# Gates and inputs at another address, and a chunk's end split differently between ScalarE and VectorE

## The chip, the cores and the metric

One core of a Trainium2 chip runs the whole program. The metric is the device time of one execution in microseconds; a kernel's time is the median of several executions. The engines are named as in the profile: PE is TensorE (matrix products; PEld its weight loads), DVE is VectorE, ACT is ScalarE, POOL is GpSimd, SP is SyncE, which issues all DMAs here. Matrix products write to PSUM, eight banks of 128 partitions by 512 float32; all other tiles lie in SBUF.

## The reference

Attention with a band mask over q, k and v (batch 4, 8 heads, 768 positions, head width 64): a query sees the first 8 positions and the 96 up to its own, a bias falls with the distance, and the softmax is taken over what is kept. The result, 3072 rows of 512, goes through a feed-forward net:

```python
h = x @ w_in                     # 3072x512 by 512x2048
g = np.maximum(0.01 * h, h)
return (g @ w_out).astype(np.float32)   # 3072x2048 by 2048x512
```

The weights are float64 at the start and all products are wanted at more than one pass's accuracy, so the kernel splits each operand into a high and a low part and adds three products: high by high, high by low, low by high.

## The kernel before, in words

The 24 blocks of 128 rows are taken in eleven chunks: two of three blocks (chunks 0 and 1) and nine of two (chunks 2 to 10). Attention runs ahead of the feed-forward net in small events (lines 192 to 330: scores, softmax, transposes, product with v). While chunks 0 and 1 run (lines 885 to 908), the weights are still being converted, into four tiles that stay for the whole program: `wih`, `wil` for the first product and `woh`, `wol` for the second.

From chunk 2 on, a chunk is eight steps p = 0 to 7, each for 256 of the 2048 hidden columns. In loop pass s the program does `hidden_pair(s)` (L449: 24 products of 256 columns with `xh`, `xl` as the moving operand and `wih`, `wil` as the weights loaded into the array), then `gates(s)`, then `out_pair(s - 2)`, the second product for the step two passes earlier (L493). `gates` copies the PSUM result to SBUF on ACT (`t`, L460), takes the leaky maximum on DVE (L461), casts the high part on ACT (`gh`, L468) and subtracts for the low part on DVE (`gl`, L469).

Where the first result lands alternates: even passes write `ps_h`, odd passes the first half of the tile `ps_p`. The second product accumulates in five banks: `bank[3]` and `bank[4]` hold the sums for the chunk's two row blocks (`bank[4]` is the second half of `ps_p`), and `bank[1]`, `bank[2]` hold four half-width partial sums of the last three steps. In the second product `gh`, `gl` are the loaded weights, and `woh`, `wol` (moving) stream through, 512 columns at a time. Steps p = 5 to 7 of chunks 3 to 10 (`fast`) do it as seven products of halves instead of eight, with sums and differences of gates (L464) and of weight halves (`h`, `l`, made once in `prepare`); these stream 256 columns, and in two products of p = 5 the first pass streams 512. The five banks are then combined in `results(c)`, called after `out_pair` of p = 7, that is in pass p = 1 of the next chunk. The next chunk's p = 0 writes `bank[3]` first and `bank[4]` three products later, in the pass after that, and has to find both read out.

All of ACT, DVE and SP work in order of their queues. In this late part the order is not pinned: a scheduler lays it out when the program is built, by a simulated time. After the last chunk, a check of the inputs (L766 to L768: a product on PE into a bank that `ps_p` had, a reduction and a cast on DVE) sets a flag, which all engines load (L923) before the program ends.

Of the kernel before, what the change touches and what calls it, by code (L numbers as in the profile page):

```python
# [10 lines left out]
F32 = mybir.dt.float32  # L11
# [7 lines left out]
P = 128  # L19
# [12 lines left out]
PAIR = 2  # L32
# [19 lines left out]
def fast_path(ctx, tc, qp, kp, vp, wi, wo, nvec, weights, nmall, out, B, H, S):  # L52
    nc = tc.nc
# [9 lines left out]
    GT = P * PAIR  # L63
# [3 lines left out]
    const = ctx.enter_context(tc.tile_pool(name="const", bufs=1))  # L67
# [11 lines left out]
    ps_x = ctx.enter_context(tc.tile_pool(name="ps_x", bufs=1, space=bass.MemoryType.PSUM))  # L79


    one = const.tile([P, 16], F32, name="one")[:, :1]
    nc.vector.memset(one, 0.0)
    pinned_exp = nc.scalar.activation(out=one, in_=one, func=AF.Exp)
    tc.keep_in_program_order(pinned_exp)
# [20 lines left out]
    def pin(ins):  # L106

        if pinned[0]:
            tc.keep_in_program_order(ins)
# [362 lines left out]
    def fast(c, p):  # L472

        return c > STD and p >= NP - FAST

    def add(o, x, y, op=ALU.add):
        pin(nc.vector.tensor_tensor(out=o, in0=x, in1=y, op=op))  # L477

    def half_bank(n):
        return bank[1 + n // 2][:, n % 2 * GT:(n % 2 + 1) * GT]  # L480

    def out_pair(s):
# [29 lines left out]
        if end:  # L512
            results(c)

    def results(c):

        u = [late["ev"].tile([P, 2, GT], F32, tag="ev", name="part") for _ in range(PAIR)]
        r = [x.rearrange("p a b -> p (a b)") for x in u]
        if not fast(c, NP - 1):
            pin(nc.scalar.copy(out=r[0], in_=bank[3]))  # L520
            pin(nc.vector.tensor_copy(out=r[1], in_=bank[4]))
        else:
            pin(nc.scalar.copy(out=u[0][:, 0], in_=half_bank(1)))
            add(u[0][:, 1], u[0][:, 0], half_bank(0))
            add(u[1][:, 0], u[0][:, 1], half_bank(3))
            add(u[1][:, 1], u[1][:, 0], half_bank(2))
            add(u[0][:, 1], u[0][:, 1], half_bank(2))
            for n in range(PAIR):
                add(r[n], r[n], bank[3 + n])
        for n in range(PAIR):  # L530
            r0 = (first_step[c] + n) * P
            nc.sync.dma_start(out=out[r0:r0 + P, :], in_=r[n])

    def prepare(p):

        e, o = 2 * p, 2 * p + 1
        first = p == NP - FAST
        h = late["w"].tile([P, (4 if first else 3) * GT], F32R, tag=f"h{p}", name=f"h{p}")
        l = late["w"].tile([P, 3 * GT], F32R, tag=f"l{p}", name=f"l{p}")
        sides[p] = h, l  # L540
        x = [y[:, n] for y in (late["ev"].tile([P, 2, GT], F32, tag="ev", name="wk") for _ in range(3)) for n in range(2)]

        def block(to, f, n):
            cs = slice(n * GT, (n + 1) * GT)
            add(to, woh[:, f, cs].bitcast(F32), wol[:, f, cs].bitcast(F32))

        def split(v, dh, dl):
            pin(nc.scalar.copy(out=dh, in_=v))
            add(dl, v, dh.bitcast(F32), ALU.subtract)
        cols = [slice(n * GT, (n + 1) * GT) for n in range(4)]  # L550
        block(x[0], e, 1)
        block(x[1], e, 0)
        add(x[2], x[0], x[1], ALU.subtract)
        split(x[2], h[:, cols[0]], l[:, cols[0]])
        block(x[1], o, 1)
        add(x[3], x[1], x[0], ALU.subtract)
        split(x[3], h[:, cols[3 if first else 2]], l[:, cols[2]])
        add(x[0], x[1], x[2], ALU.subtract)
        split(x[0], h[:, cols[1]], l[:, cols[1]])
        block(x[4], o, 0)  # L560
        add(x[5], x[4], x[0], ALU.subtract)
        split(x[5], woh[:, e, GT:], wol[:, e, GT:])
        if first:
            pin(nc.vector.memset(x[4], 0.0))
            pin(nc.scalar.copy(out=h[:, cols[2]], in_=x[4]))
# [25 lines left out]
    late = {}  # L591
# [30 lines left out]
    bank = [ps_x.tile([P, 2, 512], F32, tag="ps_t", name="ps_p")]  # L622
    bank.extend(ps_o.tile([P, 2 * GT], F32, tag="ps_o", name="ps_m") for _ in range(3))
    bank.append(bank[0][:, 1])
    for s in range(NS + 2):
        for t in ev_pair.get(s, ()):
            event(t)
        if s < NS:
            hidden_pair(s)
        if s == 0:  # L630
            ffn2(len(order) - 1)
            later.close()
            for name, n in (("a", 2), ("ev", 3), ("w", 1)):
                late[name] = ctx.enter_context(tc.tile_pool(name=name, bufs=n))
        if s < NS:
            gates(s)
        if s >= 2:
            out_pair(s - 2)
        if NP + 2 <= s < NP + 2 + 2 * FAST and s % 2 == 0:
            prepare(NP - FAST + (s - NP - 2) // 2)  # L640
# [270 lines left out]
def tile_kernel(tc, a, out, B, H, S):  # L911
    nc = tc.nc
    NF, _, NK, _ = a["wi"].shape
    DM = a["wo"].shape[3]
    NB = S // P
    with tc.tile_pool(name="keep", bufs=1) as keep, tc.tile_pool(name="xs", bufs=1, space=bass.MemoryType.DRAM) as dram:
        nvec = read_counts(tc, keep, a["ngl"])
        nmall = keep.tile([P, B * NB * H], F32, name="nmall")
        weights = (keep.tile([P, NK, NF * P], F32R, name="wih"), keep.tile([P, NK, NF * P], F32R, name="wil"),
                   keep.tile([P, NF, DM], F32R, name="woh"), keep.tile([P, NF, DM], F32R, name="wol"))  # L920
        fast_path(tc, a["qp"], a["kp"], a["vp"], a["wi"], a["wo"], nvec, weights, nmall, out, B, H, S)
        with tc.tile_pool(name="fin", bufs=1) as fin:
            flag = nc.values_load(band_holds(tc, fin, nvec, nmall), min_val=0, max_val=1,  # L923
                                  skip_runtime_bounds_check_because="the flag is a product of comparisons")
        with tc.If(flag == 0):
            xs = dram.tile([B, S // 256, P, NK, 256], F32, name="xs")
            general_attention(tc, a["qt"], a["kt"], a["vt"], nvec, xs, B, H, S)
            general_ffn(tc, weights, xs, out)
# [50 lines left out]
```

## Time and profile before

| | before |
|---|---|
| time, median of 3 | 669.3 us (668.08 to 670.57) |
| profiled execution | 667.78 us, span 666.0 us, granted clock 0.993 |
| PE busy | 630.9 us (95%) |
| DVE busy | 420.8 us (63%) |
| ACT busy | 287.9 us (43%) |
| POOL busy | 82.4 us (12%) |

The span is what the trace covers, from the first instruction to the last. Busy time of PE counts overlapping products once, and the end of a product is modelled, so the pace of products is better read from one start to the next. Three views are used beside the page: the chain of waits, which follows the work that ended last back in time and merges neighbours ("x24"); the list of who waited for whom; and the timeline of one engine, whose rows have the start in us, the duration in us, engine, line and operation, and in brackets the idle time before with what ended it.

### The profile page before, as it was taken

Reading aid. Unit: us, or ns where it says so; the run is one execution under the profiler, and the core shown is the slowest. Engines: PE = TensorE matmul, PEld = TensorE weight load, DVE = VectorE, ACT = ScalarE, POOL = GpSimd, SP = SyncE. Lnnn points to the kernel's source line nnn. Section 1 sums busy time; section 2 is a strip of 40 time slices with the busy share of each in tenths; the row PEclk is TensorE's granted clock in tenths of the full one; section 3 lists DMA queues with packets and bytes.
Section 4 is the critical chain, followed back from the end, with each engine's and each line's share of the span. In section 5 each row is a group of like instructions: output and inputs, shape, how many; then the busy total and the mean of one; then the engine's idle time right before and its main releaser. Section 6 shows DMA issues by size and latency. Waiting matters only on the chain.

```text
span 666.0 us, 15916 instructions
## 1 busy us (share of the span) xinstructions
PE 630.9 (95%) x6275; PEld 558.4 (84%) x6275; DVE 420.8 (63%) x1202; ACT 287.9 (43%) x754; POOL 82.4 (12%) x147
## 2 busy tenths in 40 slices
PE   5769999999999999899999999999999999999995
PEld 4568889998888888798889889889889889889984
DVE  5989988885657537957467556556656656534443
ACT  5877754555434434434334334334334333322221
POOL 3434600000111000101001001001001000100000
PEclk9899999999999999999999999999999999999998
DMA  8786533422555425224434433423432531400001
GB/s 281 238 257 187 184 127 126 127 64 80 175 146 197 151 75 168 62 70 156 131 95 137 144 103 94 145 88 115 142 115 84 167 103 53 131 1 1 32 1 37
DMA packets 52098, 79.76 MB, mean 120 GB/s; under 512 B 7728, under 2 KB 27184, under 8 KB 52016
## 3 DMA queue, kind: packets, MB, share of 16 engines
q1 hardware_dynamic: 52016, 78.67, 37.1%
q8 instruction: 51, 0.84, 0.5%
q14 instruction: 31, 0.25, 0.1%
HBM read 59.51 MB, written 19.14 MB: 118 GB/s over the span
## 4 chain that ended last, share of the span: by engine, by line
PE 82%; DVE 7%; ACT 3%; DMA 2%; issue 2%; POOL 1%; SPq 1%; DVEq 0%; ACTq 0%; POOLq 0%
PE ps_m L493 18%; PE ps_p L449 15%; PE ps_h L449 13%; PE ps_p L493 12%; PE ps_av L324 4%; PE ps_av L192 3%; PE ps_h L885 3%; PE ps_o L908 3%; PE ps_o L907 3%; PE ps_o L906 3%; PE ps_h L887 3%; PE ps_h L886 3%; DVE part L477 2%; DMA kr<-in_kp_dram 2%; ACT pr L219 1%
## 5 line engine op out<-in xcount | busy, mean ns | idle before, releaser
L468 ACT CAST gh<-t 128x512 fp32r<-128x512 f32 (+1 forms) x72 | 52.3, 727 | 139.0 <-PE ps_p L493 86.9
L469 DVE TENSOR_TENSOR gl<-t,gh 128x512 fp32r<-128x512 f32 (+1 forms) x72 | 59.3, 823 | 79.7 <-ACT gh L468 74.8
L219 ACT ACTIVATE pr<-pr,nmall 128x192 f32<-128x192 f32 (+1 forms) x192 | 83.3, 435 | 18.4 <-DVE nmall L206 18.4
L461 DVE SCALAR_TENSOR_TENSOR t<-t 128x512 f32<-128x512 f32 x72 | 49.6, 689 | 61.8 <-ACT t L460 61.5
L449 PE MATMUL ps_p<-xh,wih 128*128 128x256 f32 x288 | 82.7, 287 | 0.0
L449 PE MATMUL ps_h<-xh,wih 128*128 128x256 f32 x288 | 80.6, 280 | 0.0
L449 PE MATMUL ps_p<-xh,wil 128*128 128x256 f32 x288 | 80.1, 278 | 0.0
L449 PE MATMUL ps_p<-xl,wih 128*128 128x256 f32 x288 | 80.0, 278 | 0.0
L449 PE MATMUL ps_h<-xh,wil 128*128 128x256 f32 x288 | 79.7, 277 | 0.0
L449 PE MATMUL ps_h<-xl,wih 128*128 128x256 f32 x288 | 79.7, 277 | 0.0
L48 POOL TENSOR_SCALAR xh<-x 128x256 fp32r<-128x256 f32 x48 | 22.0, 457 | 466.1 <-ACT x L330 383.0
L493 PE MATMUL ps_m<-woh,gh 128*128 128x512 f32 (+1 forms) x168 | 59.0, 351 | 4.3 <-DVE part L477 4.3
L449 PEld LDWEIGHTS ps_p<-xh,wih 128*128 128x128 f32 x288 | 54.1, 188 | 6.3 <-issue 5.7
L493 PE MATMUL ps_m<-woh,gl 128*128 128x512 f32 (+1 forms) x168 | 58.1, 346 | 0.0
L493 PE MATMUL ps_m<-wol,gh 128*128 128x512 f32 (+1 forms) x168 | 58.0, 345 | 0.0
L449 PEld LDWEIGHTS ps_h<-xh,wih 128*128 128x128 f32 x288 | 54.1, 188 | 3.0 <-issue 2.2
L206 DVE CUSTOM_DVE_ANT_0 pr<-ps_av,nbw 128x192 f32<-128x192 f32 x136 | 40.5, 354 | 24.0 <-ACT x L330 23.8
L449 PEld LDWEIGHTS ps_h<-xl,wih 128*128 128x128 f32 x288 | 54.1, 188 | 0.9
L449 PEld LDWEIGHTS ps_p<-xl,wih 128*128 128x128 f32 x288 | 54.1, 188 | 0.4
L449 PEld LDWEIGHTS ps_p<-xh,wil 128*128 128x128 f32 x288 | 54.4, 189 | 0.0
L449 PEld LDWEIGHTS ps_h<-xh,wil 128*128 128x128 f32 x288 | 54.1, 188 | 0.0
L493 PE MATMUL ps_p<-woh,gh 128*128 128x512 f32 (+1 forms) x120 | 46.5, 388 | 3.3 <-ACT t L460 2.7
(130 smaller groups left out, 1467.1 us busy)
## 6 DMA issues: line engine op xcount, KB each, us to landing
via<-pr SPq DMA_DIRECT2D x30, 384.0 KB, 2.5
pt_d<-via SPq DMA_DIRECT2D x120, 96.0 KB, 2.4
kr<-in_kp_dram SPq DMA_DIRECT2D x40, 256.0 KB, 3.7
vr<-in_vp_dram SPq DMA_DIRECT2D x40, 256.0 KB, 3.2
wst<-in_wi_dram SPq DMA_DIRECT2D x16, 512.0 KB, 3.6
wst<-in_wo_dram SPq DMA_DIRECT2D x16, 512.0 KB, 3.5
qs<-in_qp_dram SPq DMA_DIRECT2D x24, 256.0 KB, 3.9
out_dram<-part SPq DMA_DIRECT2D x21, 256.0 KB, 2.3
```

The costliest lines, as they stand in the source:

```text
L48: return eng.tensor_scalar(out=dst, in0=src, scalar1=1.0, scalar2=1.0, op0=ALU.mult, op1=ALU.mult)
L192: tc.keep_in_program_order(nc.tensor.matmul(own(u, av[qf, j, a * KW:(a + 1) * KW]), lhsT=q[rows, a, qf], rhs=keys(rows, a, f), start=True, ...
L206: pin(nc.vector.tensor_tensor_reduce(out=head(u, pr, a, j), in0=own(u, ps[:, j, a * KW:(a + 1) * KW]), in1=nb, scale=-0.125, scalar=3.0e38 ...
L219: pin(nc.scalar.activation(out=p, in_=p, func=AF.Exp, scale=-1.0, bias=nm[:, 2 * a + j:2 * a + j + 1], accum_out=sm[:, 2 * a + j:2 * a + j ...
L324: tc.keep_in_program_order(nc.tensor.matmul(av[out, a, cols], lhsT=v[rows, t, j, :], rhs=near(rows, j, t, fs), start=(n == 0), stop=(n == ...
L449: tc.keep_in_program_order(nc.tensor.matmul(o, lhsT=w[:, k, fs], rhs=x[:, k, :], start=(k + i == 0), stop=(k == NK - 1 and i == 2)))
L461: pin(nc.vector.scalar_tensor_tensor(out=g, in0=g, scalar=0.01, in1=g, op0=ALU.mult, op1=ALU.max))
L468: pin(nc.scalar.copy(out=gh[:, :n - a0], in_=t[:, a0:n]))
L469: pin(nc.vector.tensor_tensor(out=gl[:, :n - a0], in0=t[:, a0:n], in1=gh[:, :n - a0].bitcast(F32), op=ALU.subtract))
L493: tc.keep_in_program_order(nc.tensor.matmul(to, lhsT=x[:, a], rhs=y, start=first and n == 0, stop=last and n == 2))
L885: tc.keep_in_program_order(nc.tensor.matmul(ps, lhsT=wih[:, k, fs], rhs=xh[:, k, :CT], start=(k == 0), stop=False))
L886: tc.keep_in_program_order(nc.tensor.matmul(ps, lhsT=wih[:, k, fs], rhs=xl[:, k, :CT], start=False, stop=False))
```

## The change

First, a chunk's end. Before, ACT copies one half bank to SBUF and DVE does the rest: four additions of 256 columns that read PSUM, then two of 512 columns that add `bank[3]` and `bank[4]`. Now ACT copies `bank[3]` (512 columns), the half bank (256) and `bank[4]` (512), in this order in the text, and DVE does six additions of 256 columns, four of them with a PSUM operand, and one of 512 in SBUF. A third tile `u` is used beside the two result tiles.

Second, addresses. The first small tile of the pool `const` grows from 64 to 128 bytes a partition, which moves what is allocated after it from the same side by 64 bytes; `gap`, 64 bytes, moves the tiles `h`, `l` back. The addresses in the two built programs, modulo 128 bytes:

| tile | before | after |
|---|---|---|
| `wih`, `wil`, `woh`, `wol` | 0 | 0 |
| `xh`, `xl` of chunk 0 | 0 | 64 |
| `xh`, `xl` of chunks 1 to 10 | 64 | 64 |
| `gh`, `gl`, all chunks | 0 | 64 |
| `h`, `l` of `prepare` | 0 | 0 |
| q, k, v, `pr` of attention | 64 | 0 |
| `pt`, `dg` of attention | 0 | 64 |
| `pt_d` of attention | 64 | 64 |

```diff
-    one = const.tile([P, 16], F32, name="one")[:, :1]
+    one = const.tile([P, 32], F32, name="one")[:, :1]
 ...
     def results(c):
 
-        u = [late["ev"].tile([P, 2, GT], F32, tag="ev", name="part") for _ in range(PAIR)]
-        r = [x.rearrange("p a b -> p (a b)") for x in u]
+        r = [late["ev"].tile([P, 2, GT], F32, tag="ev", name="part") for _ in range(PAIR)]
+        rows = [x.rearrange("p a b -> p (a b)") for x in r]
+        pin(nc.scalar.copy(out=rows[0], in_=bank[3]))
         if not fast(c, NP - 1):
-            pin(nc.scalar.copy(out=r[0], in_=bank[3]))
-            pin(nc.vector.tensor_copy(out=r[1], in_=bank[4]))
+            pin(nc.vector.tensor_copy(out=rows[1], in_=bank[4]))
         else:
-            pin(nc.scalar.copy(out=u[0][:, 0], in_=half_bank(1)))
-            add(u[0][:, 1], u[0][:, 0], half_bank(0))
-            add(u[1][:, 0], u[0][:, 1], half_bank(3))
-            add(u[1][:, 1], u[1][:, 0], half_bank(2))
-            add(u[0][:, 1], u[0][:, 1], half_bank(2))
-            for n in range(PAIR):
-                add(r[n], r[n], bank[3 + n])
+            u = late["ev"].tile([P, 2, GT], F32, tag="ev", name="u")
+            pin(nc.scalar.copy(out=u[:, 0], in_=half_bank(1)))
+            pin(nc.scalar.copy(out=rows[1], in_=bank[4]))
+            add(r[0][:, 0], r[0][:, 0], u[:, 0])
+            add(u[:, 0], u[:, 0], half_bank(0))
+            add(u[:, 1], u[:, 0], half_bank(3))
+            add(u[:, 0], u[:, 0], half_bank(2))
+            add(r[1][:, 1], r[1][:, 1], half_bank(2))
+            add(r[0][:, 1], r[0][:, 1], u[:, 0])
+            add(r[1], r[1], u[:, 1].unsqueeze(1).to_broadcast([P, 2, GT]))
         for n in range(PAIR):
             r0 = (first_step[c] + n) * P
-            nc.sync.dma_start(out=out[r0:r0 + P, :], in_=r[n])
+            nc.sync.dma_start(out=out[r0:r0 + P, :], in_=rows[n])
 
     def prepare(p):
 
         e, o = 2 * p, 2 * p + 1
         first = p == NP - FAST
+        if first:
+            gap = late["w"].tile([P, 16], F32, tag="gap", name="gap")
+            nc.gpsimd.memset(gap, 0.0)
```

The scheduler lays out the late part anew. This is ACT at the end of chunk 3 (`part` are the result tiles, `t`, `gh` the gates of the next chunk, `ps_m` any of `bank[1]` to `bank[3]`), before:

```order
L460 COPY t<-ps_p 128x512
L523 COPY part<-ps_m 128x256
L468 CAST gh<-t 128x512
L460 COPY t<-ps_h 128x512
L468 CAST gh<-t 128x512
```

and after:

```order
L460 COPY t<-ps_p 128x512
L468 CAST gh<-t 128x512
L519 COPY part<-ps_m 128x512
L524 COPY u<-ps_m 128x256
L525 COPY part<-ps_p 128x512
L460 COPY t<-ps_h 128x512
L468 CAST gh<-t 128x512
```

The three copies stand behind the cast `gh` of pass p = 1 and ahead of the copy `t` of pass p = 2. On DVE at the same place, before:

```order
L461 SCALAR_TENSOR_TENSOR t<-t 128x512
L477 TENSOR_TENSOR part<-part,ps_m 128x256
L250 STREAM_TRANSPOSE pr<-pr 128x768
L477 TENSOR_TENSOR part<-part,ps_m 128x256
L469 TENSOR_TENSOR gl<-t,gh 128x512
L477 TENSOR_TENSOR part<-part,ps_m 128x256 x2
L477 TENSOR_TENSOR part<-part,ps_p 128x512
L477 TENSOR_TENSOR part<-part,ps_m 128x512
L461 SCALAR_TENSOR_TENSOR t<-t 128x512
```

and after:

```order
L461 SCALAR_TENSOR_TENSOR t<-t 128x512
L250 STREAM_TRANSPOSE pr<-pr 128x768
L469 TENSOR_TENSOR gl<-t,gh 128x512
L477 TENSOR_TENSOR part<-part,u 128x256
L477 TENSOR_TENSOR u<-u,ps_m 128x256 x3
L477 TENSOR_TENSOR part<-part,ps_m 128x256
L461 SCALAR_TENSOR_TENSOR t<-t 128x512
L477 TENSOR_TENSOR part<-part,u 128x256
L477 TENSOR_TENSOR part<-part,u 128x512
```

No addition reads `bank[3]` or `bank[4]` any more, and two additions now follow the next pass's L461. At the very end of the program, after the last chunk, DVE had (`row` is the check's product, `fl` and `flag` its reduction and cast):

```order
L477 TENSOR_TENSOR part<-part,ps_m 128x256 x4
L477 TENSOR_TENSOR part<-part,ps_p 128x512
L477 TENSOR_TENSOR part<-part,ps_m 128x512
L767 TENSOR_REDUCE fl<-row 1x1
L768 CAST flag<-fl 1x1
```

and has now:

```order
L477 TENSOR_TENSOR part<-part,u 128x256
L477 TENSOR_TENSOR u<-u,ps_m 128x256
L773 TENSOR_REDUCE fl<-row 1x1
L477 TENSOR_TENSOR u<-u,ps_m 128x256
L774 CAST flag<-fl 1x1
L477 TENSOR_TENSOR u<-u,ps_m 128x256
L477 TENSOR_TENSOR part<-part,ps_m 128x256
L477 TENSOR_TENSOR part<-part,u 128x256
L477 TENSOR_TENSOR part<-part,u 128x512
```

The reduction has moved between the additions. Its product `row` on PE writes where `ps_p` was and so waits for the last reader of that tile, which is now ACT's copy of `bank[4]`. On ACT the three copies stand alone at this end, `bank[3]` first.

## The prediction

> **What bounds the kernel now.** I read the page first, then who waited for whom, then the chain of waits around a chunk's end, then the timelines of the engines there and at the program's end.
>
> ```profile
> PE 630.9 (95%) x6275; PEld 558.4 (84%) x6275; DVE 420.8 (63%) x1202; ACT 287.9 (43%) x754; POOL 82.4 (12%) x147
> PE 82%; DVE 7%; ACT 3%; DMA 2%; issue 2%; POOL 1%; SPq 1%; DVEq 0%; ACTq 0%; POOLq 0%
> ```
>
> PE is the bound: it is busy for 95% of the span and makes 82% of the chain that ended last. Time is won by stopping its waits, or by a shorter step from one product to the next. The waits in the late part have two rows:
>
> ```profile
> PE ps_m L493 <- DVE part L477: 4.3, 6, 0.7
> PE ps_p L493 <- ACT t L460: 2.7, 2, 2.4
> ```
>
> The first is the chunk's end that the change rewrites, six times 0.7 us. The second, a write to the second half of `ps_p` behind ACT's copy of the first, is untouched. Here is one of the six, in the chain of waits at the end of chunk 3 (start us, us, what):
>
> ```profile
> 312.13 0.38 PE ps_m L493 x3
> ...
> 313.07 0.38 DVE part L477
> 313.45 0.60 DVE gl L469
> 314.05 1.87 DVE part L477 x4
> ...
> 315.96 0.96 PE ps_m L493 x3
> 316.92 0.70 PE ps_p L493 x3
> 317.62 0.70 PE ps_m L493 x3
> ```
>
> The chunk's last products end near 312.5, and the chain then goes to DVE, which alternates additions of the old chunk with `gl` of the new one. PE's products run on meanwhile, until:
>
> ```profile
> 314.96 0.28 PE L449 MATMUL ps_h<-xh,wil 128*128 128x256 f32 x1
> 315.96 0.50 PE L493 MATMUL ps_m<-woh,gh 128*128 128x512 f32 x1 [0.72 <-DVE part L477]
> 316.30 0.39 PE L493 MATMUL ps_m<-wol,gh 128*128 128x512 f32 x1
> ```
>
> The step from the first to the second is 1.00 us where 0.11 is usual, a loss of 0.89; the next step is 0.34 where 0.23 is usual (0.70 for three, above), since the loading of the weights waited too. One stall costs 0.89 + 0.11 = 1.0 us.
>
> **Part one: the stall, and what frees the banks now.** PE waits for `bank[3]` first and for `bank[4]` three products (0.7 us) later. Both are now read by ACT alone. What ACT does there before:
>
> ```profile
> 310.74 0.37 ACT L523 COPY part<-ps_m 128x256 f32<-128x256 f32 x1
> 312.40 0.62 ACT L468 CAST gh<-t 128x512 fp32r<-128x512 f32 x1 [1.29 <-PE ps_m L493]
> 315.33 0.59 ACT L460 COPY t<-ps_h 128x512 f32<-128x512 f32 x1 [2.30 <-PE ps_h L449]
> ```
>
> A copy of 512 columns out of PSUM is 0.59, one of 256 is 0.37. The new copies follow the cast, which ends at 313.0: `bank[3]` is free at 313.6, the half bank at 314.0, `bank[4]` at 314.6. PE asks for them at 315.07 and 315.8. So the stall goes, with 1.4 us to spare on the first bank. ACT's extra 1.2 us a chunk lies in the 2.3 us that it idled before L460; without that cover, the copy `t` behind it would come late by what is missing, and after it L461 and `gl`, which are wanted two passes later. On DVE, five additions (about 2.0 us, from 313.7) end just before L461 can start at 315.9, and the last two follow it. Six stalls: **-5.9 us** (from 4.3 by the waits row alone to 6.0 by starts). The program's end (below) has no next chunk, and chunks 2 and 9 have no such wait.
>
> **Part two: the end of the program.** There the same copies are on the path. Before:
>
> ```profile
> 656.34 1.72 DVE L477 TENSOR_TENSOR part<-part,ps_m 128x256 f32<-128x256 f32 x4 [1.65 <-ACT part L523]
> 657.40 0.28 PE L493 MATMUL ps_m<-woh,gl 128*128 128x256 f32 x1
> 658.57 0.68 DVE L477 TENSOR_TENSOR part<-part,ps_m 128x512 f32<-128x512 f32 x1
> 658.68 0.96 SPq L532 DMA_DIRECT2D out_dram<-part  x2
> 658.71 0.27 PE L766 MATMUL row<-ident,fl 128*1 128x128 f32 x1 [1.03 <-DVE part L477]
> 659.17 0.27 DVE L767 TENSOR_REDUCE fl<-row 1x1 f32<-1x128 f32 x1
> ```
>
> The half banks were finished early, so four additions were nearly done when the last product ended at 657.7, and the last addition ended at 659.25. Now everything is behind ACT's copy of `bank[3]`, which holds the last product: that copy to 658.3, the half bank to 658.6, `bank[4]` to 659.1. DVE starts at 658.6; a dependent addition of 256 takes 0.43 (1.72 for four), one that depends on nothing near 0.34. First addition 658.6, second 659.05; then the reduction, which waits for `row`, which waits for the copy of `bank[4]`: 659.1, and 0.46 from PE's start to DVE's as above, so 659.6, with its 0.27. Then three more PSUM additions, the cast and one in SBUF to 661.4, and the one of 512 (0.68) to 662.1. SP issues the last row and loads the flag behind it, so the program ends later by 662.1 - 659.25 = **+2.8 us**. Bounds: 2.0, if the additions run at 0.34 and none waits for the reduction; 3.5, if each waits for the one before.
>
> **Part three: the addresses.** The trace has no row for the gates at 64, so I look for pairs of rows with the same shape at the two distances between moving operand and loaded weights. 256 columns, chain of waits: `xh` (64 off) against `wih`, and the second product of a fast step (all at 0):
>
> ```profile
> 443.24 2.73 PE ps_h L449 x24
> 448.74 2.83 PE ps_p L449 x24
> ...
> 458.45 1.78 PE ps_m L493 x15
> ```
>
> Per product: 2.73/24 = 113.8 ns, in some passes 117.9, against 1.78/15 = 118.7 with both at 0. 384 columns, twelve products, from the first to the next operation, chunk 1 (64 off) and then chunk 0 (both at 0):
>
> ```profile
> 114.50 0.18 PE ps_h L885
> ...
> 116.62 0.23 PE ps_o L906
> ...
> 172.40 0.18 PE ps_h L885
> ...
> 174.51 0.23 PE ps_o L906
> ```
>
> 2.12/12 = 176.7 ns at 64, 2.11/12 = 175.8 at 0: no gain, if anything 0.9 ns lost. So the two widths disagree, and the 256-column pair differs in more than the address. 512 columns exist at 0 only: 232 ns (0.70 for three). How many there are, from the groups kept apart by shape:
>
> ```profile
> L906 PE MATMUL ps_o<-woh,gh 128*128 128x512 f32 x96 | 37.9, 394 | 0.0
> L493 PE MATMUL ps_m<-woh,gh 128*128 128x512 f32 x96 | 38.7, 403 | 4.3 <-DVE part L477 4.3
> L493 PE MATMUL ps_m<-woh,gh 128*128 128x256 f32 x72 | 20.4, 283 | 0.0
> ```
>
> Of 512 columns there are nine groups of 96 and one of 16: 880. Of 256 in the second product, 488. Of 384 in chunk 0, 192. Best case, all at the pace of 113.8 ns for 256 columns: 512 columns in 227.6 (-4.4 x 880 = -3.9 us), 256 in 113.8 (-4.9 x 488 = -2.4), 384 in 170.7 (-5.1 x 192 = -1.0): -7.3 us. Worst case, as the 384-column pair: +0.9 x 192 and, scaled by width, +1.2 x 880 and +0.6 x 488: +1.5 us. I take for 256 columns, whose nearest rows are those of 113.8 to 117.9 ns, 114.5 (-4.2 x 488 = -2.0), and for 512, where as at 384 the load covers only a part of the product, a fifth of the best (-0.8): **-2.8 us**.
>
> The Trainium skill speaks against this part: "SBUF — State Buffer", section "Who interferes with whom", and "TensorE: Matmul & The Clock Gate", part 2, say that the moving operand and the weight load have read ports of their own and that PE waits on nobody there. By that the third part would be nothing. The 384-column pair agrees with it, the 256-column pair (113.8 against 118.7 ns) does not.
>
> The rest is small. POOL's `memset` of 16 columns runs once, in an engine busy 12%. The tiles of attention move too; for them I have no pair of rows and take nothing. SP's two result DMAs now stand together behind DVE's last addition, which ends near 317.5 (L461 from 315.9, then 256 and 512 columns), with the next loads of k and v behind them as before.
>
> **Sum.** -5.9 + 2.8 - 2.8 = -5.9 us. The profiled execution's own time is 667.78 us, 1.8 over its span of 666.0; it would become 661.9. It was 1.5 below the median of the runs, so I forecast from the median: 669.3 - 5.9, say **663.4 us**.
>
> **Rivals.**
>
> *The address is worth its best case*: every product runs at the pace of the 24 in 2.73 us. For it: that pace holds over most passes of L449. Against it: the 384-column pair. -5.9 + 2.8 - 7.3 = -10.4, 658.9 us.
>
> *The address is worth nothing*, and the 256-column difference comes from the fast steps' own changes of operand every three products. For it: the 384-column pair. -5.9 + 2.8 = -3.1, 666.2 us. That is within 0.5%, since the program's end takes back half of what the stalls gave. It is where the rule of the Trainium skill above would lead.
>
> *The stall stays and only the end is paid.* Place: ACT's queue at a chunk's end. The copy of `bank[3]` stands behind `gh`, which waits for the last product before it can overwrite its buffer; if ACT then holds more than 1.4 us of other work before that copy (an event's four exponentials would), or the copy waits for an earlier output DMA to leave its buffer, PE finds the bank unread as before. Against it: the order has nothing between cast and copies, and the buffers' last DMAs are a whole chunk old. With the address at its worst: 0 + 2.8 + 1.5 = +4.3, 673.6 us; with the address at nothing, 672.1.
>
> **How the numbers follow.** Forecast 0.44, best-case address 0.20, no address effect 0.27, stall stays 0.09. The range 658 to 668 us holds the first three with their bounds and leaves out the last and the edge of the second. About 0.5% (3.3 us, below 666.0 or above 672.6) is what a measurement tells from no change: faster takes the forecast, the best case and a small part of the third, 0.68; slower 0.08; within, 0.24.
>
> **What would show it.** Right: no wait of L493 for DVE's `part` and starts of `ps_m` 0.11 us after the 24th product; ACT copies of 0.59, 0.37, 0.59 us ending before L460 of the next pass; a last addition that ends 4.7 us after the last product's start instead of 1.9; 24 products of 2.73 us unchanged and the fast steps' 15 in about 1.72; three of 512 columns near 0.69. Wrong: three of 512 in 0.68 (best case) or still 0.70 with 15 in 1.78 (nothing); a new wait of L493 for ACT `part`; `t` of L460 late at the first pass after the copies; or a wait that takes the gained microsecond back within the same chunk, such as the one for ACT's `t`, which I leave as it is.

## The result, and the profile after

| | before | after |
|---|---|---|
| time, median of 4 | 669.34 us (668.08 to 670.57) | 662.32 us (659.95 to 663.91) |
| profiled execution | 667.78 us, span 666.0 | 659.95 us, span 658.2 |
| granted clock | 0.993 | 0.988 |

The ratio is 0.9892, with a 95% interval of 0.9856 to 0.9929: the change is faster, by 7.0 us of the medians. In a later batch on one chip with other kernels the change had 662.20 against 668.81 us, 0.9904 (0.9874 to 0.9933). The forecast was 663.4. One run of the kernel before, at 1032.61 us and a granted clock of 0.562 in the batch of the first experiments, is left out of every difference here.

The first rows of the page after, and those on the chain of the work that ended last:

```profile
PE 626.5 (95%) x6275; PEld 557.0 (85%) x6275; DVE 423.9 (64%) x1210; ACT 294.9 (45%) x770; POOL 82.3 (13%) x148
...
DVE 0%; DVEq 0%
DVE part L477 0%; DVEq L929 0%
```

PE is still the bound with the same 6275 products; 4.4 us less of it is counted as busy. The chain is of no use here, since it breaks off after two pieces at the program's end. So I read waits and timelines. Of the list of who waited for whom, the two rows of the late part:

```profile
PE ps_p L493 <- ACT t L460: 2.3, 1, 2.3
...
PE row L772 <- ACT part L525: 1.4, 1, 1.4
```

No row of L493 for DVE's `part` is left, where there were six waits and 4.3 us; nor has one for ACT's `part` come. Of the two waits for `t` one (near 389 us before) is gone too. PE at the end of chunk 3, on its timeline, the same products as at 314.96 and 315.96 before:

```profile
313.64 0.28 PE L449 MATMUL ps_h<-xh,wil 128*128 128x256 f32 x1
313.76 0.39 PE L493 MATMUL ps_m<-woh,gh 128*128 128x512 f32 x1
...
314.45 0.39 PE L493 MATMUL ps_p<-woh,gh 128*128 128x512 f32 x1
```

The step is 0.12 us instead of 1.00, and three products of 512 columns take 0.69 us. What ACT and then DVE do there:

```profile
311.63 0.58 ACT L519 COPY part<-ps_m 128x512 f32<-128x512 f32 x1
312.11 0.38 ACT L524 COPY u<-ps_m 128x256 f32<-128x256 f32 x1
312.37 0.60 ACT L525 COPY part<-ps_p 128x512 f32<-128x512 f32 x1
314.01 0.59 ACT L460 COPY t<-ps_h 128x512 f32<-128x512 f32 x1 [1.04 <-PE ps_h L449]
```

```profile
314.23 0.41 DVE L477 TENSOR_TENSOR part<-part,ps_m 128x256 f32<-128x256 f32 x1
314.63 0.69 DVE L461 SCALAR_TENSOR_TENSOR t<-t 128x512 f32<-128x512 f32 x1
```

`bank[3]` is free at 312.21, 1.55 us before PE asks for it; ACT still idles 1.04 us before `t`; and DVE's L461 starts at 314.63, 0.03 after `t` is there. Nothing that was added is late.

The end of the program:

```profile
647.78 0.28 PE L493 MATMUL ps_m<-woh,gl 128*128 128x256 f32 x1
648.09 0.58 ACT L519 COPY part<-ps_m 128x512 f32<-128x512 f32 x1 [4.12 <-PE ps_m L493]
...
650.37 0.13 DVE L774 CAST flag<-fl 1x1 int32<-1x1 f32 x1
...
651.14 1.02 DVE L477 TENSOR_TENSOR part<-part,u 128x256 f32<-128x256 f32 x2
651.62 1.11 SPq L535 DMA_DIRECT2D out_dram<-part  x2
```

The last addition ends at 652.16, 4.38 us after the start of the last product, where it was 1.85. The last row holds two additions of two shapes.

**Where the time went.** The chunks 4 to 9 hold the six waits and nothing of the program's start or end, so they serve as the measure from here on: from the first product of chunk 4 to the first of chunk 10, before and then after.

```profile
300.32 0.38 PE L449 MATMUL ps_h<-xh,wih 128*128 128x256 f32 x1
...
608.12 0.28 PE L449 MATMUL ps_h<-xh,wih 128*128 128x256 f32 x1
```

```profile
298.97 0.38 PE L449 MATMUL ps_h<-xh,wih 128*128 128x256 f32 x1
...
598.97 0.28 PE L449 MATMUL ps_h<-xh,wih 128*128 128x256 f32 x1
```

307.80 became 300.00 us: -7.80. With the same kind of rows elsewhere the spans' difference of -7.84 splits as: first product of chunk 0, +1.1 (attention's start; it lies between 43.0 and 45.9 us over all the kernels here, and none of them changes it on purpose); chunks 0 and 1, -1.9; chunks 2 and 3, -0.6; chunks 4 to 9, -7.8; chunk 10, -0.5; from the last product to the end of the span, +1.8 (8.61 to 10.40).

### The profile page after: what moved, and what is told of

Its sections match the earlier page's. It is cut to its first block, busy times and chain, and to the rows that moved or that the text cites. A ratio compares the mean times of both kernels' runs of the same rounds, so it can differ in the third digit from the quotient of the medians.

```text
span 658.2 us, 15933 instructions
## 1 busy us (share of the span) xinstructions
PE 626.5 (95%) x6275; PEld 557.0 (85%) x6275; DVE 423.9 (64%) x1210; ACT 294.9 (45%) x770; POOL 82.3 (13%) x148
## 5 line engine op out<-in xcount | busy, mean ns | idle before, releaser
L461 DVE SCALAR_TENSOR_TENSOR t<-t 128x512 f32<-128x512 f32 x72 | 49.5, 688 | 59.9 <-ACT t L460 59.4
L449 PE MATMUL ps_p<-xh,wih 128*128 128x256 f32 x288 | 82.4, 286 | 0.0
L449 PE MATMUL ps_h<-xh,wih 128*128 128x256 f32 x288 | 80.9, 281 | 0.0
L449 PE MATMUL ps_h<-xl,wih 128*128 128x256 f32 x288 | 80.0, 278 | 0.0
L449 PE MATMUL ps_h<-xh,wil 128*128 128x256 f32 x288 | 79.9, 277 | 0.0
L449 PE MATMUL ps_p<-xl,wih 128*128 128x256 f32 x288 | 79.9, 277 | 0.0
L449 PE MATMUL ps_p<-xh,wil 128*128 128x256 f32 x288 | 79.8, 277 | 0.0
L449 PEld LDWEIGHTS ps_p<-xh,wih 128*128 128x128 f32 x288 | 54.1, 188 | 6.3 <-issue 5.7
L493 PE MATMUL ps_m<-woh,gl 128*128 128x512 f32 (+1 forms) x168 | 58.0, 345 | 0.0
L493 PE MATMUL ps_m<-wol,gh 128*128 128x512 f32 (+1 forms) x168 | 57.7, 343 | 0.0
L493 PE MATMUL ps_m<-woh,gh 128*128 128x512 f32 (+1 forms) x168 | 57.7, 343 | 0.0
L449 PEld LDWEIGHTS ps_h<-xh,wih 128*128 128x128 f32 x288 | 54.2, 188 | 3.0 <-issue 2.2
L449 PEld LDWEIGHTS ps_h<-xl,wih 128*128 128x128 f32 x288 | 54.1, 188 | 0.8
L449 PEld LDWEIGHTS ps_p<-xl,wih 128*128 128x128 f32 x288 | 54.1, 188 | 0.5
L449 PEld LDWEIGHTS ps_h<-xh,wil 128*128 128x128 f32 x288 | 54.1, 188 | 0.0
L449 PEld LDWEIGHTS ps_p<-xh,wil 128*128 128x128 f32 x288 | 54.1, 188 | 0.0
L493 PE MATMUL ps_p<-woh,gh 128*128 128x512 f32 (+1 forms) x120 | 46.3, 385 | 3.1 <-ACT t L460 2.3
```

The source lines that it names most:

```text
L449: tc.keep_in_program_order(nc.tensor.matmul(o, lhsT=w[:, k, fs], rhs=x[:, k, :], start=(k + i == 0), stop=(k == NK - 1 and i == 2)))
L461: pin(nc.vector.scalar_tensor_tensor(out=g, in0=g, scalar=0.01, in1=g, op0=ALU.mult, op1=ALU.max))
L493: tc.keep_in_program_order(nc.tensor.matmul(to, lhsT=x[:, a], rhs=y, start=first and n == 0, stop=last and n == 2))
```

## The experiments

### The two parts apart

The first kernel has the new `results` and the addresses of before; the second has the addresses alone.

```diff
 # new results, old addresses: the change, but
-    one = const.tile([P, 32], F32, name="one")[:, :1]
+    one = const.tile([P, 16], F32, name="one")[:, :1]
-        if first:
-            gap = late["w"].tile([P, 16], F32, tag="gap", name="gap")
-            nc.gpsimd.memset(gap, 0.0)
 # addresses alone: the kernel before, but
-    one = const.tile([P, 16], F32, name="one")[:, :1]
+    one = const.tile([P, 32], F32, name="one")[:, :1]
+        if first:
+            gap = late["w"].tile([P, 16], F32, tag="gap", name="gap")
+            nc.gpsimd.memset(gap, 0.0)
```

> The new chunk's end alone, all addresses as before. My theory: the six stalls go (-5.9 us) and the program's end costs +1.8 us of span, so about 4 us below before, 665.2 us; products of 512 columns stay at 232 ns and those of 256 in the second product at 119 ns. Rival, all of the gain is the addresses: no change or +2 us, 669 to 671 us. Rival, the stalls give more than I took because later chunks start earlier too: 663 us or less.

> The new addresses alone, the chunk's end as before. My theory: about 3.5 to 4 us below before (512 columns from 232 to near 230 ns, 256 columns from 119 to 116, 384 columns from 176 to 174), with the six stalls of 1.0 us still there: 665.5 us. Rival, the address does nothing and the shorter steps seen after the change come with the other order of work: 669.3 us and steps of 232 and 119 ns.

Measured: new `results` alone 664.46 us, ratio 0.9926 (0.9908 to 0.9943); addresses alone 665.67 us, ratio 0.9937 (0.9917 to 0.9956). Chunks 4 to 9 of the first kernel and of the second:

```profile
301.52 0.38 PE L449 MATMUL ps_h<-xh,wih 128*128 128x256 f32 x1
...
602.95 0.28 PE L449 MATMUL ps_h<-xh,wih 128*128 128x256 f32 x1
```

```profile
300.30 0.38 PE L449 MATMUL ps_h<-xh,wih 128*128 128x256 f32 x1
...
606.49 0.28 PE L449 MATMUL ps_h<-xh,wih 128*128 128x256 f32 x1
```

301.43 and 306.19 us, so -6.37 and -1.61, together -7.98 where the change has -7.80. Both parts work, and here they add up. With the new `results` alone no wait of L493 for `part` is left; with the addresses alone its row is the old one:

```profile
PE ps_m L493 <- DVE part L477: 4.4, 6, 0.8
```

The first kernel's -6.37 is six times 1.0 us and about 0.3 for the small wait near 389 us, which is gone in this kernel too and still there in the second. In the profiles, before that wait ACT starts `t` 0.36 us after PE's last product has ended, after the change 0.09; why is open.

By the medians the parts give -5.3 and -4.0 us, together -9.3, more than the change's -6.6 to -7.0. That is no contradiction in the mechanism, since the chunks 4 to 9 add up within 0.2 us. What lies outside them scatters by 1 to 3 us between executions (the start of attention, above, and the clock in chunk 3, below).

### The last chunk combined as before

```diff
     def results(c):
 
+        if c == NCHUNK - 1:
+            u = [late["ev"].tile([P, 2, GT], F32, tag="ev", name="part") for _ in range(PAIR)]
 ...  # the combination of the kernel before, then
+            return
```

> The change, but the last chunk alone is combined as before (ACT copies the half bank, DVE adds the two outer banks out of PSUM). My theory: the span after the last product's start falls from 10.4 to 8.6 us, so 1.8 us below the changed kernel, 660.5 us. Rival, the end is set by the flag and the branch and not by the additions: 662.3 us, and the span after the last product stays 10.4 us.

It ran twice, the second time on one chip with the change:

> The change with the last chunk combined as in the kernel before, once more, on one chip with the change itself. Theory (the new combination costs 1.5 to 2.0 us where no next chunk hides it): 659.5 to 660.5, 1.5 to 2.0 us under the change of the same batch. Rival (the program's end is hidden behind the writing of the last rows): within 0.5 us of it.

> The change itself, to stand beside the others of this batch. Both theories: 662 +- 1.5 us.

Measured: 659.26 us, ratio 0.9852 (0.9826 to 0.9878), then 659.96, 0.9869 (0.9840 to 0.9898), beside the change's 662.20. It beats both kernels. The end in the second run:

```profile
648.60 0.28 PE L493 MATMUL ps_m<-woh,gl 128*128 128x256 f32 x1
649.19 0.68 DVE L477 TENSOR_TENSOR part<-part,ps_p 128x512 f32<-128x512 f32 x1
649.79 0.68 DVE L477 TENSOR_TENSOR part<-part,ps_m 128x512 f32<-128x512 f32 x1
...
650.69 0.14 DVE L788 CAST flag<-fl 1x1 int32<-1x1 f32 x1
```

The last addition ends 1.87 us after the last product's start again. The span ends 8.64 us after that start, in the change of the same batch 10.05: 1.4 us. The rest of the 2.2 us between the medians lies in the scatter named above: chunks 4 to 9 take 299.99 us in both. Over all profiles but that of the kernel with DVE copies (below), the span ends 8.40 to 8.79 us after that start with the old combination (five executions) and 10.05 to 10.40 with the new one (five), 1.55 us apart in the mean. DVE's last addition comes 2.5 us earlier with the old one, so the end does not move with that addition alone.

Where the other microsecond goes, the traces show in rows that the views leave out, those of SP's load of the flag and of its branch. In all these executions SP issues the last row, then loads the flag and branches. It branches 3.10 us after the last product's start before, and 5.74 us (5.63 in the second profile) in the change: 2.5 to 2.6 us later. But its next instruction comes 3.2 to 3.6 us behind the branch with the old combination and only 2.5 to 2.75 us behind it with the new one. With the old one all five engines load the flag within 0.04 us, behind the cast, which is DVE's last operation; with the new one the cast is done at 650.50 in the first profile, ahead of the last additions, and the other four engines branch 1.4 to 2.4 us ahead of SP. Whether that shortens SP's stretch is open, since no run moved the flag alone. It is not the transfer of the last rows that SP waits for there: in every execution they have landed before that next instruction.

### The addresses: which distance counts

Three kernels move tiles alone. In the first, `h` and `l` go to 64 with the gates; in the second every weight goes to 64, so that no distance is left, in L449 neither; in the third the gates stand 32 bytes off.

```diff
 # h, l at 64: the change without gap
-        if first:
-            gap = late["w"].tile([P, 16], F32, tag="gap", name="gap")
-            nc.gpsimd.memset(gap, 0.0)
 # no distance: the kernel before, with the weights 64 bytes on
-        nmall = keep.tile([P, B * NB * H], F32, name="nmall")
+        nmall = keep.tile([P, B * NB * H + 16], F32, name="nmall")[:, :B * NB * H]
 # 32 bytes: the change with
-    one = const.tile([P, 32], F32, name="one")[:, :1]
+    one = const.tile([P, 24], F32, name="one")[:, :1]
-            gap = late["w"].tile([P, 16], F32, tag="gap", name="gap")
+            gap = late["w"].tile([P, 24], F32, tag="gap", name="gap")
```

> The change without the 64 bytes of gap, so that the prepared halves h, l lie at 64, as gh, gl do, while woh, wol stay at 0. If the distance between moving operand and loaded weights is what counts, the products of 256 columns that stream h or l go back from 116 towards 119 ns and those that stream woh or wol stay at 116; by 272 such products that is 0.8 us. If the address of gh, gl alone counts, all stay at 116 ns.

> The kernel before, with every weight moved by 64 bytes: weights, gates, tokens and the attention values all stand at 64 modulo 128, and no product has a distance left, those of the first layer of 256 columns (L449) included, which had 64 in the kernel before. Theory (the distance between moving operand and loaded weights modulo 128 sets the pace): the products of 256 columns in L449 go from 114.7 to about 118.8 ns, and 1690 of them cost +7 us, so about 676.5 us; three products of 512 columns stay at 0.70 us. Rival (the absolute address of the moving operand sets it, 64 being good): the second products get the change's pace (three of 512 columns in 0.69), L449 stays, and the time falls by 4 to about 665.5. Rival (addresses do nothing, the paces come from something else in the change): 669 to 670.

> The change with 32 bytes in place of 64: the gates of all chunks but the first, and the first chunk's tokens, stand 32 bytes off the weights modulo 128. Theory A (any distance from the weights will do): the paces of the change, three products of 512 columns in 0.69 us, 660 to 663 us. Theory B (it must be half of 128, as if two halves of a line were served apart): the paces of the kernel before, 0.70 us for three, about 664.5 us. Theory C (in proportion): half of the gain, about 662 to 663 us.

By the built programs two addresses are other than these texts say: with no distance, q, k, v and `pr` of attention stand at 0, as they do in the change; and with 32 bytes the gates of the first chunk stand at 32 like the others.

Measured: `h`, `l` at 64: 660.13 us, one execution. No distance: 674.49 us, ratio 1.0082 (1.0054 to 1.0109), slower than before by 5.7 us where the theory had 7. 32 bytes: 663.52 us, one execution. Single executions scatter by more than these effects, so the chunks 4 to 9 serve again: 300.32 us with `h`, `l` at 64 and 301.78 with 32 bytes, where the change has 300.00 and the new `results` with the old addresses 301.43. The paces, from PE's timeline. First the 21 products of 256 columns of one fast step in chunk 5 (seven with `h`, `l`, and `woh`, `wol`, all three passes), from the first to the next pass: before, after, with `h`, `l` at 64, and with 32 bytes.

```profile
361.76 0.28 PE L493 MATMUL ps_m<-h,gh 128*128 128x256 f32 x1
...
364.27 0.28 PE L449 MATMUL ps_h<-xh,wih 128*128 128x256 f32 x1
```

```profile
359.14 0.28 PE L493 MATMUL ps_m<-h,gh 128*128 128x256 f32 x1
...
361.53 0.28 PE L449 MATMUL ps_h<-xh,wih 128*128 128x256 f32 x1
```

```profile
359.14 0.28 PE L493 MATMUL ps_m<-h,gh 128*128 128x256 f32 x1
...
361.64 0.28 PE L449 MATMUL ps_h<-xh,wih 128*128 128x256 f32 x1
```

```profile
361.24 0.28 PE L493 MATMUL ps_m<-h,gh 128*128 128x256 f32 x1
...
363.75 0.28 PE L449 MATMUL ps_h<-xh,wih 128*128 128x256 f32 x1
```

2.51, 2.39, 2.50 and 2.51 us, or 119.5, 113.8, 119.0 and 119.5 ns each. Then the first product's 24 of one pass, and the 12 of 512 columns behind it, before, and the 24 with no distance:

```profile
391.58 0.28 PE L449 MATMUL ps_h<-xh,wih 128*128 128x256 f32 x1
394.31 0.39 PE L493 MATMUL ps_m<-woh,gh 128*128 128x512 f32 x1
397.08 0.28 PE L449 MATMUL ps_p<-xh,wih 128*128 128x256 f32 x1
```

```profile
394.84 0.28 PE L449 MATMUL ps_h<-xh,wih 128*128 128x256 f32 x1
397.68 0.39 PE L493 MATMUL ps_m<-woh,gh 128*128 128x512 f32 x1
```

2.73 us became 2.84, 113.8 ns 118.3. Over the whole program, as the mean step from one start to the next of every product that no wait follows (steps under 137, 205 and 274 ns for the three widths), in ns, with the distance modulo 128 in brackets:

| products | before | after | `h`, `l` at 64 | no distance | 32 bytes |
|---|---|---|---|---|---|
| first, 256 columns (1690) | 114.7 (64) | 114.6 (64) | 114.3 (64) | 118.7 (0) | 114.3 (64) |
| second, 256, `h`, `l` (200) | 118.6 (0) | 116.3 (64) | 119.6 (0) | 118.6 (0) | 119.3 (32) |
| second, 256, `woh`, `wol` (275) | 119.3 (0) | 116.1 (64) | 118.3 (64) | 119.2 (0) | 119.9 (32) |
| second, 512, `woh`, `wol` (790) | 232.2 (0) | 229.7 (64) | 229.9 (64) | 232.6 (0) | 233.1 (32) |
| first, 384, chunk 0 (176) | 175.8 (0) | 174.0 (64) | 174.7 (64) | 176.1 (0) | 174.6 (32) |
| first, 384, chunk 1 (192) | 176.3 (64) | 173.6 (64) | 174.1 (64) | 176.0 (0) | 173.3 (64) |

The change's second profile gives, from the top, 114.7, 116.3, 116.1, 230.1, 174.6 and 174.1, so differences up to 0.6 ns are scatter.

What follows. It is the distance between the two operands, not the address of either: with everything at 64 the second product is as before and the first one, which loses its distance, gets as slow as the second (+4.0 ns; 1690 of them make 6.8 us, and the chunks 4 to 9 went from 307.80 to 311.40 although the six waits were 0.2 us shorter each). The cleanest pair is this kernel and the one with the addresses alone: the operands named here stand at the same places modulo 128 in both but for the weights with `h` and `l`, 64 bytes on, and the paces are 118.7 against 114.6 ns in the first product and 232.6 against 229.5 in the second of 512 columns. For 256 and 512 columns it has to be 64: 32 bytes give nothing. The 384-column rows do not fit: at 32 bytes chunk 0 has the better pace, and chunk 1, whose operands stood 64 bytes apart in all but one of these kernels, went from 176.3 to 173.6 without a move of its own. It goes with the gates of the second products between which it runs: 176.3 with gates at 0, in the new `results` alone too, and 173.3 to 174.1 with gates at 32 or 64 and the weights at 0. Other tiles moved together with the gates, so that the gates do it is not shown. The `woh`, `wol` products of 256 columns point the same way: 118.3 ns, and not the expected 116, where the `h`, `l` products beside them had lost their distance. How a pace would pass from one group to the next is open.

The Trainium skill gives PE a read port of its own for the moving operand and one for the weight load ("SBUF — State Buffer", section "Who interferes with whom"). The runs here differ from what follows from it: with nothing but addresses moved against the change, the pace of the fast step above went from 113.8 to 119.0 and 119.5 ns.

### DVE instead of ACT

```diff
-        pin(nc.scalar.copy(out=rows[0], in_=bank[3]))
+        pin((nc.vector.tensor_copy if fast(c, NP - 1) else nc.scalar.copy)(out=rows[0], in_=bank[3]))
 ...
-            pin(nc.scalar.copy(out=rows[1], in_=bank[4]))
+            pin(nc.vector.tensor_copy(out=rows[1], in_=bank[4]))
```

> The change, but DVE instead of ACT copies the two outer banks at a chunk's end, ahead of its other work there; ACT keeps the copy of the half bank. Theory (what removes the six waits is that the outer banks are read first, whichever engine reads them): no wait of L493 for part at the chunks' ends, chunk to chunk as in the change, and at the program's end about 1 us more, since two copies of 0.69 us join DVE's additions there: 662 to 664 us. Rival (it is DVE's queue that keeps PE waiting, and only ACT can free the banks in time): a wait of L493 for DVE's part again in each of six chunks, up to 1 us each, so 664 to 669 us.

Measured: 664.55 us, one execution. DVE at the end of chunk 3, and its last operations of the program:

```profile
314.55 0.65 DVE L519 COPY part<-ps_m 128x512 f32<-128x512 f32 x1
315.13 0.67 DVE L525 COPY part<-ps_p 128x512 f32<-128x512 f32 x1
315.73 0.67 DVE L469 TENSOR_TENSOR gl<-t,gh 128x512 fp32r<-128x512 f32 x1
```

Chunks 4 to 9 take 300.00 us here too (302.14 to 602.14), and L493 has no wait for `part`. So it is enough that the outer banks are read first; that ACT does it is not what removes the waits. `gl` comes 1.2 us later behind the copies, and nobody waits for it. At the program's end it does cost: the last product starts at 650.94 and the span ends 11.77 us later, against 10.05 in the change, since all nine operations there now stand in one queue. Its profile also has 1.5 us more in chunk 3, and that is the clock:

### A half clock after the one long wait that is left

No kernel was made for this; it shows in four of eleven profiled executions (new `results` alone, no distance, DVE copies, and the first of the two with the last chunk as before; the second of these has it not). PE's timeline of the kernel with DVE copies, behind the wait for `t` in chunk 3:

```profile
273.35 0.51 PE L493 MATMUL ps_p<-woh,gh 128*128 128x512 f32 x1 [2.09 <-ACT t L460]
...
274.63 0.39 PE L493 MATMUL ps_m<-woh,gl 128*128 128x512 f32 x1
274.86 0.59 PE L493 MATMUL ps_p<-woh,gh 128*128 128x512 f32 x1
275.24 0.63 PE L493 MATMUL ps_p<-wol,gh 128*128 128x512 f32 x1
275.67 0.63 PE L493 MATMUL ps_p<-woh,gl 128*128 128x512 f32 x1
...
278.23 0.32 PE L449 MATMUL ps_h<-xl,wih 128*128 128x256 f32 x1
```

The step goes from 0.23 to 0.43 us at 274.9 and comes back at 278.3. The trace also records when the clock changed: here at 25.72, 32.55, 42.79, 46.20, 274.90 and 278.31 us. The times between changes are multiples of 3.413 us, and so they are in every trace up to the program's end: the clock changes on a grid, whose place differs between executions of one kernel. Two stretches of that grid (busy time of PE, PEld, DVE, ACT and POOL, then the granted clock):

```profile
271.49:274.90 3.41, 1.55 (x7) 1.27 (x8) 3.38 (x13) 2.42 (x10) 0.00 (x0) 1.00 0.00 0
274.91:278.30 3.39, 3.39 (x15) 3.10 (x14) 3.39 (x9) 1.02 (x2) 0.00 (x0) 0.50 0.19 71
```

And the change of the second batch, its wait on PE's timeline and the two stretches on which it lies:

```profile
273.68 0.50 PE L493 MATMUL ps_p<-woh,gh 128*128 128x512 f32 x1 [2.08 <-ACT t L460]
```

```profile
269.50:272.89 3.39, 2.09 (x16) 1.62 (x14) 3.36 (x15) 2.10 (x10) 1.09 (x2) 1.00 0.18 63
272.91:276.31 3.40, 2.63 (x13) 2.25 (x14) 3.40 (x14) 1.81 (x5) 0.00 (x0) 1.00 0.00 0
```

So it matters how the wait falls on the grid. In the four executions 1.82 to 2.08 us of it lay in one stretch, PE was busy for 1.33 to 1.60 us of that stretch, and the next one ran at half clock. In the other seven the wait straddled two stretches, and the clock stayed full; PE was busy for 1.88 us or more of the emptier one, except in the second execution with the last chunk as before, with 1.57 us and 1.83 us of the wait. So neither number separates the two kinds fully, and eleven executions don't give the rule. The same wait of some 2.1 us costs 1.3 to 1.6 us more when it falls that way: chunk 3 took 54.47 us with DVE copies and 54.35 in the first execution with the last chunk as before, against 52.91 to 53.04 in the change and 52.92 in the second.

## Why the prediction was right, point by point

**The stall** (-5.9 us): right in mechanism and size. The new `results` alone took 6.37 us off the chunks 4 to 9, six times 1.0 and the rest mostly another wait. The 1.4 us to spare on the first bank were 1.55, and L461 started right behind `t`, as worked out. What I had as untouched, the writes behind ACT's `t`, was so for the long one only; the short one went with the new `results`, which nothing in my steps gave.

**The end of the program** (+2.8): right in mechanism, too large. The last addition was put at 4.7 us behind the last product's start and came at 4.38. SP's load of the flag and its branch moved with it as the steps had it, by 2.5 to 2.6 us. But the span ended only 1.8 us later by the first profile and 1.4 by the second, below the lower bound of 2.0: I took everything behind the flag's load to last as long as before, and it became shorter (5.51 us from SP's branch to the span's end before, 4.66 and 4.42 after). Why is open; the order had shown that the flag's cast now stands ahead of the last additions, and I did not ask what that does to the other engines. Putting the old combination back at that one place gave the 1.4 us back.

**The addresses** (-2.8): right in sign, too small. From the table, before to after: 2.5 ns x 880 products of 512 columns, 2.8 x 488 of 256 (between the two rows), 1.8 x 192 and 2.7 x 192 of 384: 2.2 + 1.4 + 0.3 + 0.5 = -4.4 us, and -3.9 by the change's second profile. The term for 256 columns, 114.5 ns and -2.0, was too hopeful (116.2 and -1.4, since not every step runs at 113.8). The one for 512, a fifth of the best case, was too timid: -2.2 against -0.8. And 384 columns, which I left out since one pair of rows showed no gain at 64, gained 0.8: that pair (chunk 1 at 176.7, chunk 0 at 175.8) was no fair one, because chunk 1 ran between second products that had no distance, with which its pace seems to go. The rival of no effect, where the Trainium skill's rule on the ports would lead, falls with the addresses alone at 0.9937; the best case falls with paces that stay above it for every width.

**The sum** (-5.9) was near the measured -7.0 partly by compensation: the addresses gave 1.1 to 1.6 more, the small wait 0.3, the end cost 1.0 to 1.4 less, and what is then too much, 1.3 to 2.2 us, is within the scatter of the start and of chunk 3. Since only one execution before was profiled, that scatter can't be split further. The fourth case, that the stall stays behind other work of ACT, falls with the 1.04 us that ACT still idled there.

## What to carry to other kernels

When a bank is wanted again soon, read it out first with one plain copy and add later from SBUF; which engine copies matters little while its queue has room, but where no next work hides the additions, at the program's end, keep the version that finishes early (1.4 us here). And see how the moving operand and the loaded weights of a product lie to each other modulo 128 bytes: 64 apart was 1 to 3% faster here than 0 apart, at no cost but an unused strip, and 32 was not for products of 256 and 512 columns. To judge such small terms, measure a stretch that holds none of the scatter: 300 us of chunks agreed within 0.02 us over five executions of three kernels whose times differed by up to 5.5.

## What the runs showed of the hardware that was not expected

The pace of PE depends on the distance of its two SBUF operands modulo 128 bytes: 118.7 ns at 0 or 114.7 at 64 for 256 columns of the first product, 232.2 or 229.7 for 512 of the second; it seems to depend on that of the neighbouring products too. And PE's clock was halved for one stretch of 3.413 us after a wait of some 2 us, when nearly all of the wait fell into a single stretch of the grid on which the clock changes (one execution of eleven had it so and kept the full clock). The Trainium skill ("TensorE: Matmul & The Clock Gate", part 1) puts that fall at an idle window of about 3.4 us that runs free of the kernel. The grid of 3.413 us in these traces agrees with the free-running window; that the window has to be idle does not, since PE was busy for 1.33 to 1.60 us of the stretch before each fall in chunk 3.
